# The decay chain of a complex linear attention: the multiply im/re moved to VectorE, a clamp dropped, the 1e-6 term taken into the log scan, the phase rounded on ScalarE

## The chip, the cores and the metric

The kernel runs on one core of a Trainium2 chip. The metric is the device time of one execution in microseconds (us), the median of several runs. The core has four compute engines with a queue each, worked off in order: TensorE (PE; its weight loads are listed as PEld), VectorE (DVE), ScalarE (ACT) and GpSimd (POOL). SyncE (SP) issues the DMAs. Engines wait for each other by semaphores.

## What is computed

The input is a linear attention with a complex decay for every position, head and dimension (batch 4, 8 heads, 768 positions, dimension 48), followed by a soft mixture of 8 experts and a last layer with a squared ReLU. The part that matters here is the decay:

```python
mag = np.sqrt(a_re * a_re + a_im * a_im)
scale = np.minimum(mag, 0.999) / (mag + 1e-06)
a_re_n, a_im_n = (a_re * scale, a_im * scale)
for t in range(S):
    new_re = ar * S_re - ai * S_im
    new_im = ar * S_im + ai * S_re
    S_re, S_im = (new_re + kv, new_im)
    y[:, :, t] = np.einsum('bhd,bhde->bhe', q[:, :, t], S_re)
```

Then x = y with the heads side by side, logits = x @ phi, a softmax over tokens and one over slots, the experts between them, and relu(x @ w_in)**2 @ w_out.

## The kernel before, in words

**The factored form.** The product of the decays up to a position is written as exp(L) times a rotation by an angle. L is the running sum of log(min(mag, 0.999)/(mag + 1e-6)*mag), the angle the running sum of arctan(im/re). With E = exp(+-L) and W = (cos, sin) of the angle, queries and keys are scaled and rotated once, and the recurrence becomes chunks of 128 positions: scores, a causal mask, a product with v, and a state carried from chunk to chunk. Three flags tell at the end if all decays were in the range of this form; if not, the function `general` runs the recurrence step by step. On these inputs it doesn't run.

**The work.** There are 24 units (u) of 128 positions: 4 batches of 6. The decays are prepared in T groups (v), with dimensions times heads on the partitions and 3 tiles side by side: nine groups, of 1, 2 and 3 units, then six of 3. A group of 3 units works on 128x1152 elements. Its steps are the *T chain* of `plan_t` (lines 797 to 873), in this order: clamp re (D, line 823), Ln (A), Exp with a minus sign, which gives 1/re (A, with a flag), im times 1/re (G, line 826), clamp that to +-1.56 (D, line 827), square (A, line 828), Ln(1+x) (A), square of the square for a flag (A, line 830, aside), log of the magnitude as a weighted sum (D, line 831), 1e-6/magnitude by an Exp (A, line 832), minimum with log 0.999 less that term (D, line 833), running sum L in three scans, held above -65 (D, line 838 through line 836), Arctan (A), running sum of the angle in three scans (D, line 841 through line 836), whole turns as an integer (D, line 843), angle less the turns (D, lines 846 to 849). D, A and G stand for VectorE, ScalarE and POOL. Activations go through the helpers at lines 276 and 291, so these two lines stand for all of them in the profile.

`spans` and `waves` then turn L and the angle by TensorE (line 882), so that positions lie on the partitions, and take Exp, Sin and cos. `plan_u` does a unit: scale q and k by E (line 965, "decay"), rotate them by W (line 971), transpose (line 989), scores (line 1037), mask (line 1041), products with v and the state (lines 1052 and 1057), new state (lines 1014 to 1026). Beside these run the slot sums (`plan_g`) and the conversion of w_in from float64 (`plan_wi`). After it come the experts (lines 527 and 542), then the last layer (lines 660 to 742).

**What sets the order.** In this first part all steps are handed to the class `Plan` (lines 84 to 161), a list scheduler that runs while the program is built. Each step has an engine, a cost, a due time, the steps that it comes after and the buffers that it takes and gives back. The planner plays the engines forward with these costs; of the steps that could start on an engine it issues the one due first. What it issues is the fixed order of each engine's queue on the chip. Some copies may go to ScalarE or VectorE ("AD"); the planner gives them to whichever takes them first, with a late due time on VectorE. Where TensorE has nothing in the plan and two of six PSUM banks are free, it adds a pair of warm-up products (line 1170).

The T chain's due times start at the unit's place, less 1.2 times the sum of the chain's costs, less 10 us, and grow by 1.2 times each step's cost. To each is added a shift from the table `SHIFT`, found by the step's number in the chain and by its group:

```python
D3 = 3 * (0.00104 * w + 0.07)
i = add(eng, cst, start, fn, after=after, ..., tab=kw.get("tab"), key=f"T{k}")
start += cst * SLACK
```

The shifts that matter here: T3 -129.1, T4 -23.5, T5 19.7, T6 26.0, T7 32.2, T8 -43.6, T9 5.8, T10 -193.4, T11 4.8, T12 17.9, T13 25.5, T14 17.2, T15 -1.6; "decay" 8.4. Of the 16 expert weight loads 3 are issued early; the others wait for the buffers that the last T group, the last turn and the last unit give back (lines 1144 to 1152).

Of the kernel before, what the change touches and what calls it, by code (L numbers as in the profile page):

```python
# [11 lines left out]
F32 = mybir.dt.float32  # L12
# [26 lines left out]
AR_MIN, AR_MAX, X_LIM, L_MIN = 1e-5, 1e18, 1.56, -65.0  # L39
# [3 lines left out]
# how much later than their place in the order the steps of a name, or of a T unit, are due  # L43
# [40 lines left out]
class Plan:  # L84
    """Steps of one engine each, issued in the order of a list schedule: a step starts when
    the steps before it are through and its buffers are free, and of those that could start,
    the one due first does. Steps that need another function table count as due HOLD later.
    A step of two engines runs on the one that takes it first, as due SECOND later on the second."""
# [6 lines left out]
    def add(self, eng, cost, due, fn, after=(), get=(), put=(), lat=0.0, tab=None, key=None):  # L95
        """cost: of each of the engines. fn takes the engine where there is a choice."""
        engs = [eng] if eng in ("PE", "SP") else list(eng)
        key = key or fn.__name__
        due += SHIFT.get(key, 0.0) + SHIFT.get(self.group, 0.0)
        self.steps.append((dict(zip(engs, cost if len(engs) > 1 else [cost])), due, fn,  # L100
                           [a for a in after if a is not None], get, put, lat, tab))
        return len(self.steps) - 1

    def issue(self, warm):
# [3 lines left out]
        ready = {"SP": [], "D": [], "A": [], "G": [], "PE": []}  # L108
# [55 lines left out]
def general(ctx, tc, raw, cs, phs, grp, table):  # L164
    """The recurrence step by step, for any decays; then the slot sums again."""
    nc = tc.nc
# [86 lines left out]
def moe_kernel(ctx, tc, raw, cst, aT, qk, vv_d, phi, w1, w2, w_in, w_out, out):  # L253
# [16 lines left out]
    lim = const.tile([128, 2], F32, name="lim")  # L270
# [22 lines left out]
    def grp_steps(g, st, p_s, ps_m):  # L293
        """Slot sums and slot weights of four units: (engine, cost, what, wants) each."""
# [75 lines left out]
    def merge_steps(p_s, ps_m):  # L370
        """The four running slot sums as one, over the sum of the weights."""
# [59 lines left out]
    def combine_steps(p_m):  # L431
        """The slot weights of all tokens from their logits."""
        m = p_m.tile([128, NU], F32, name="m")
        wide = lambda: m.unsqueeze(2).to_broadcast([128, NU, NS])

        def inverse():
            V.tensor_reduce(out=m, in_=cn, axis=AX, op=ALU.add)
            V.tensor_scalar(out=m, in0=m, scalar1=1e-9, scalar2=None, op0=ALU.add)
            V.reciprocal(m, m)
        return [lambda: V.tensor_reduce(out=m, in_=cn, axis=AX, op=ALU.max),  # L440
                lambda: (V.tensor_tensor(out=cn, in0=cn, in1=wide(), op=ALU.subtract), tact(SET_EXP, cn, cn, AF.Exp)),
                inverse,
                lambda: V.tensor_tensor(out=cn, in0=cn, in1=wide(), op=ALU.mult)]
# [5 lines left out]
    def f64_steps(p_d, raw, dst):  # L449
        """float64 as pairs of words (low, high) to float32: (engine, what) each."""  # L450
        shape = list(dst.shape)
        t = {}

        def word(k):
            return raw()[:, :, :, k]

        def fields():
            t["x"] = p_d.tile(shape, U32, name="dx")
            V.tensor_scalar(out=t["x"], in0=word(1), scalar1=3, scalar2=0x3FFFFFF8, op0=ALU.logical_shift_left, op1=ALU.bitwise_and)

        def size():
            t["y"] = p_d.tile(shape, F32, name="dy")
            act(t["y"], word(1).bitcast(F32), AF.Abs)

        def low():
            V.scalar_tensor_tensor(out=t["x"], in0=word(0), scalar=29, in1=t["x"], op0=ALU.logical_shift_right, op1=ALU.bitwise_or)

        def top():
            V.scalar_tensor_tensor(out=t["x"], in0=word(1), scalar=0xC0000000, in1=t["x"], op0=ALU.bitwise_and, op1=ALU.bitwise_or)

        def flush():
            V.scalar_tensor_tensor(out=dst, in0=t["y"], scalar=F64_MIN, in1=t["x"].bitcast(F32), op0=ALU.is_ge, op1=ALU.mult)
        return [("A", size), ("D", fields), ("D", low), ("D", top), ("D", flush)]
# [6 lines left out]
    # expert weights, in the order in which the products take them: of four experts, a quarter  # L480
    # of the hidden columns each
# [11 lines left out]
    def grp_flags(p_f, ps_f):  # L493
        """128 when all decays are in the range of the factored form."""
# [10 lines left out]
    def finish(weights, psum, ps_b, hid, p_raw, p_d, used, swap, check):  # L505
        """The experts on the slot sums, then the last layer. used(n): product n has taken its weights;
        swap: makes room for the last layer's weights when the sixth up product has taken its own."""
# [42 lines left out]
        def warm(n):  # L550
            """Products that keep the array's clock up."""
            for _ in range(n):
                mm(ph_[0][:, :C], ident, ident, start=True, stop=True)
# [28 lines left out]
        def decode(n):  # L582
            """The n-th rows of w_out as float32."""
            R["dw", n] = R["dw"].tile([128, 1, DM], F32, name="dw")
            return [fn for _, fn in f64_steps(p_d, lambda: R["raw", n], R["dw", n])]

        def part(n):
            """The n-th rows of w_out as two parts."""
# [161 lines left out]
    with tc.manual_schedule():  # L750
# [46 lines left out]
        def plan_t(v):  # L797
# [5 lines left out]
            A1, D1, D2, P1 = cost("A", e), cost("D", e), cost("D", e, half=True), e * 0.00223  # L803
            D3 = 3 * (0.00104 * w + 0.07)
# [21 lines left out]
            step("G", P1, lambda: nc.gpsimd.tensor_tensor(out=g("a1"), in0=g("a1"), in1=g("t2"), op=ALU.mult))  # L826
            step("D", D2, lambda: V.tensor_scalar(out=g("a1"), in0=g("a1"), scalar1=X_LIM, scalar2=-X_LIM, op0=ALU.min, op1=ALU.max))
# [5 lines left out]
            step("D", D1, lambda: V.scalar_tensor_tensor(out=g("a0"), in0=g("a0"), scalar=LN_CLIP, in1=g("t3"), op0=ALU.min, op1=ALU.subtract))  # L833
            def sums(out, src, op, low, first):
                for j in range(3):
                    V.tensor_tensor_scan(out=v3(out)[:, j], data0=v3(src)[:, j], data1=low.to_broadcast([128, w]),  # L836
                                         initial=first[:, j:j + 1] if first is not None else 0.0, op0=ALU.add, op1=op)
            step("D", D3, lambda: sums(g("t3"), g("a0"), ALU.max, lim[:, :1], None), put=["a0"], key=("L", v))

            step("A", A1, lambda: tact(SET_TRIG, g("a1"), g("a1"), AF.Arctan), mid=("sq", v), tab=SET_TRIG)  # L840
            step("D", D3, lambda: sums(new("t4"), g("a1"), ALU.add, lim[:, 1:], st.pop(("fl", v - 1)) if c else None),
                 get=["t4"], dep=("fl", v - 1))
            step("D", D2, lambda: V.tensor_scalar(out=g("a1").bitcast(I32), in0=g("t4"), scalar1=1.0 / (2 * math.pi), scalar2=None, op0=ALU.mult))
# [15 lines left out]
            for k, (eng, cst, fn, kw) in enumerate(seq):  # L859
# [4 lines left out]
                if eng == "G":  # L864
                    after.append(ids["a1", v])
# [26 lines left out]
        def spans(v, due):  # L892
            """E+ and E- of the units of v, and the decay over all of v."""
# [210 lines left out]
        V.memset(lim[:, :1], L_MIN)  # L1104
        V.memset(lim[:, 1:], 0.0)
# [76 lines left out]
        def used(k):  # L1182
            supply(n + N_POST + k)
# [65 lines left out]
```

## Time and profile before

| | us |
|---|---|
| three runs | 581.35, 582.32, 584.56; median 582.32 |
| profiled execution: span from its first to its last instruction | 578.5 |
| TensorE busy | 540.0 (93%) |
| VectorE busy | 453.5 (78%) |
| ScalarE busy | 373.7 (65%) |
| POOL busy | 44.7 (8%) |

The times of the runs include what lies around the span; of the profiled execution only the span is known. An engine counts as busy while an instruction of its own runs, so an instruction that is held up by another engine's use of memory also counts as busy. A window row gives, for a stretch, the busy us of each engine with the number of instructions in brackets, then the share of TensorE's full clock that was granted, and the DMA's share.

### The profile page before, as it was taken

Reading aid. Unit: us, or ns where it says so; the run is one execution under the profiler, and the core shown is the slowest. Engines: PE = TensorE matmul, PEld = TensorE weight load, DVE = VectorE, ACT = ScalarE, POOL = GpSimd, SP = SyncE. Lnnn points to the kernel's source line nnn. Section 1 sums busy time; section 2 is a strip of 40 time slices with the busy share of each in tenths; the row PEclk is TensorE's granted clock in tenths of the full one; section 3 lists DMA queues with packets and bytes.
Section 4 is the critical chain, followed back from the end, with each engine's and each line's share of the span. In section 5 each row is a group of like instructions: output and inputs, shape, how many; then the busy total and the mean of one; then the engine's idle time right before and its main releaser. Section 6 shows DMA issues by size and latency. Waiting matters only on the chain. (4 is left out here: it accounts for less than half of the span.)

```text
span 578.5 us, 10970 instructions
## 1 busy us (share of the span) xinstructions
PE 540.0 (93%) x4368; PEld 473.5 (82%) x4368; DVE 453.5 (78%) x743; ACT 373.7 (65%) x687; POOL 44.7 (8%) x28
## 2 busy tenths in 40 slices
PE   2989999999998989999999997789999999999995
PEld 2978788878787878887844987679999999999995
DVE  3979899999999999998648799866666666666662
ACT  6878788889798868783214678455555555555552
POOL 1111020012001020000000133210000000000000
PEclk9989899999999989999999998899999999999998
DMA  8762323343415223498996133010010100100101
GB/s 308 292 249 83 109 87 120 117 131 113 134 42 159 77 68 111 134 390 320 386 374 228 54 110 110 1 55 1 1 55 1 54 2 1 56 0 2 55 1 60
DMA packets 24827, 67.29 MB, mean 116 GB/s; under 512 B 2240, under 2 KB 15424, under 8 KB 22720
## 3 DMA queue, kind: packets, MB, share of 16 engines
q1 hardware_dynamic: 24768, 66.51, 33.3%
q8 instruction: 36, 0.59, 0.4%
q14 instruction: 23, 0.19, 0.1%
HBM read 61.78 MB, written 4.72 MB: 115 GB/s over the span
## 5 line engine op out<-in xcount | busy, mean ns | idle before, releaser
L727 PE MATMUL po<-woh,sh 128*128 128x384 f32 x384 | 131.7, 343 | 5.7 <-ACT sh L276 5.7
L727 PE MATMUL po<-wol,sh 128*128 128x384 f32 x384 | 130.6, 340 | 0.0
L276 ACT ACTIVATE sh<-s 128x512 fp32r<-128x512 f32 x96 | 60.6, 632 | 71.6 <-DVE s L684 71.2
L695 DVE TENSOR_TENSOR sl<-s,sh 128x512 fp32r<-128x512 f32 x81 | 56.1, 693 | 55.6 <-ACT sh L276 34.7
L724 PE MATMUL po<-woh,sl 128*128 128x384 f32 x384 | 86.8, 340 | 0.7 <-POOLq L1192 0.7
L727 PEld LDWEIGHTS po<-woh,sh 128*128 128x128 f32 x384 | 73.0, 190 | 9.1 <-ACT sh L276 8.4
L727 PEld LDWEIGHTS po<-wol,sh 128*128 128x128 f32 x384 | 72.9, 190 | 3.8
L684 DVE TENSOR_TENSOR s<-s 128x512 f32<-128x512 f32 x85 | 60.0, 706 | 14.6 <-ACT s L276 14.5
L724 PEld LDWEIGHTS po<-woh,sl 128*128 128x128 f32 x384 | 69.5, 189 | 1.3 <-POOLq L1192 1.1
L276 ACT ACTIVATE s<-ph 128x512 f32<-128x512 f32 x96 | 56.9, 593 | 17.6 <-PE ph L680 17.3
L276 ACT ACTIVATE T<-pt 96x512 f32<-96x512 f32 x81 | 45.3, 592 | 19.5 <-PE pt L989 19.0
L1170 PE MATMUL pt<-cs 128*128 128x128 f32 x284 | 41.9, 300 | 11.7 <-DMA cs<-in_const_dram 11.5
L1037 PE MATMUL pt<-T,T 96*128 96x128 f32 x384 | 52.0, 282 | 0.0
L1170 PEld LDWEIGHTS pt<-cs 128*128 128x128 f32 x284 | 38.1, 211 | 13.9 <-DMA cs<-in_const_dram 11.5
L1037 PEld LDWEIGHTS pt<-T,T 96*128 96x128 f32 x384 | 46.2, 192 | 3.5 <-issue 3.0
L1052 PE MATMUL py<-am,v 128*48 128x128 f32 x384 | 41.4, 294 | 2.5 <-DVE am L1041 2.5
L680 PE MATMUL ph<-cT,G 128*128 128x512 f32 x96 | 40.0, 416 | 0.3 <-ACT s L276 0.2
L826 POOL TENSOR_TENSOR a<-a,t 128x1152 f32<-128x1152 f32 (+2 forms) x9 | 24.3, 2699 | 183.5 <-ACT t L291 167.4
L836 DVE TENSOR_TENSOR_SCAN t<-a,lim 128x384 f32<-128x384 f32 (+2 forms) x39 | 36.7, 995 | 0.2 <-ACT a L291 0.2
L1041 DVE TENSOR_TENSOR am<-pt,cs 128x512 f32<-128x512 f32 x48 | 32.7, 682 | 4.3 <-PE pt L1037 3.7
L695 POOL TENSOR_TENSOR sl<-s,sh 128x512 fp32r<-128x512 f32 x15 | 20.2, 1347 | 151.6 <-ACT sh L276 146.6
L1057 PE MATMUL py<-T,S 96*48 96x128 f32 x320 | 31.9, 277 | 0.0
(155 smaller groups left out, 936.2 us busy)
## 6 DMA issues: line engine op xcount, KB each, us to landing
w<-in_w_dram SPq DMA_DIRECT2D x16, 1536.0 KB, 9.3
qk<-in_qk_dram SPq DMA_DIRECT2D x24, 384.0 KB, 3.2
a<-in_a_dram SPq DMA_DIRECT2D x14, 576.0 KB, 4.1
raw<-in_wi_dram SPq DMA_DIRECT2D x16, 384.0 KB, 4.4
raw<-in_wo_dram SPq DMA_DIRECT2D x16, 384.0 KB, 3.2
v<-in_vn_dram SPq DMA_DIRECT2D x24, 192.0 KB, 2.4
out_dram<-o SPq DMA_DIRECT2D x24, 192.0 KB, 2.0
a<-in_a_dram SPq DMA_DIRECT2D x2, 384.0 KB, 6.0
```

What stands on the lines that cost most here:

```text
L276: return nc.scalar.activation(*args, **kw)
L680: mm(p, G[:, 128 * f:128 * (f + 1)], R["cT", g], start=True, stop=True)
L684: V.tensor_tensor(out=s, in0=s, in1=s, op=ALU.mult)
L695: (nc.gpsimd if 0 < n < 16 else V).tensor_tensor(out=sl, in0=s, in1=sh, op=ALU.subtract)
L724: mm(po[t][:, :DM], sl[:, C * t:C * (t + 1)], R["woh"][:, f], start=False, stop=f == 15)
L727: mm(po[t][:, :DM], sh[:, C * t:C * (t + 1)], R[w][:, f], start=f == 0 and w == "woh", stop=False)
L836: V.tensor_tensor_scan(out=v3(out)[:, j], data0=v3(src)[:, j], data1=low.to_broadcast([128, w]), initial=first[:, j:j + 1] if first is not ...
L1037: mm(p[:, C * h:C * (h + 1)], st["T", u, 1, g][:, h], st["T", u, 0, g][:, h], start=True, stop=True)
L1041: V.tensor_tensor(out=m, in0=st["pa", u, g].rearrange("p (h t) -> p h t", h=4), in1=cs[:, C_CAUS:C_CAUS + C].unsqueeze(1).to_broadcast([12 ...
L1052: mm(p[64 * w:64 * w + D, C * pr:C * (pr + 1)], st["v", u][:, h], st["am", u, h // 4][:, h % 4], start=True, stop=fst)
L1057: mm(p[64 * w:64 * w + D, C * pr:C * (pr + 1)], st["S", u][:, h], st["T", u, 0, h // 4][:, h % 4], start=False, stop=True)
L1170: mm(p[:, :C], ident, ident, start=True, stop=True)
```

## The change

The multiply im * (1/re) is a VectorE instruction instead of POOL's. The clamp of the quotient to +-1.56 is gone; values out of that range are told by the flag of the fourth power, as before. The term 1e-6/magnitude is no longer subtracted together with the minimum; the minimum is a one-input instruction, and the scan of the logs subtracts the term as its second operation, reading it from the tile that it writes (in place of the lower limit of -65). The whole turns are computed by a ScalarE copy with a scale and an integer output. The planner's cost of a scan is changed, and its queue for POOL and the constant tile with the limits go. The chain has 15 steps in place of 16, so the later steps have other numbers; the table `SHIFT` is as it was.

```diff
-AR_MIN, AR_MAX, X_LIM, L_MIN = 1e-5, 1e18, 1.56, -65.0
+AR_MIN, AR_MAX = 1e-5, 1e18
...
-        ready = {"SP": [], "D": [], "A": [], "G": [], "PE": []}
+        ready = {"SP": [], "D": [], "A": [], "PE": []}
...
-            A1, D1, D2, P1 = cost("A", e), cost("D", e), cost("D", e, half=True), e * 0.00223
-            D3 = 3 * (0.00104 * w + 0.07)
+            A1, D1, D2 = cost("A", e), cost("D", e), cost("D", e, half=True)
+            D3 = 3 * (0.0021 * w + 0.05)
...
-            step("G", P1, lambda: nc.gpsimd.tensor_tensor(out=g("a1"), in0=g("a1"), in1=g("t2"), op=ALU.mult))
-            step("D", D2, lambda: V.tensor_scalar(out=g("a1"), in0=g("a1"), scalar1=X_LIM, scalar2=-X_LIM, op0=ALU.min, op1=ALU.max))
+            step("D", D1, lambda: V.tensor_tensor(out=g("a1"), in0=g("a1"), in1=g("t2"), op=ALU.mult), needs=("a1", v))
...
-            step("D", D1, lambda: V.scalar_tensor_tensor(out=g("a0"), in0=g("a0"), scalar=LN_CLIP, in1=g("t3"), op0=ALU.min, op1=ALU.subtract))
-            def sums(out, src, op, low, first):
+            step("D", D2, lambda: V.tensor_scalar(out=g("a0"), in0=g("a0"), scalar1=LN_CLIP, scalar2=None, op0=ALU.min))
+
+            def sums(out, src, op, less, first):
                 for j in range(3):
-                    V.tensor_tensor_scan(out=v3(out)[:, j], data0=v3(src)[:, j], data1=low.to_broadcast([128, w]),
+                    V.tensor_tensor_scan(out=v3(out)[:, j], data0=v3(src)[:, j], data1=less(j),
                                          initial=first[:, j:j + 1] if first is not None else 0.0, op0=ALU.add, op1=op)
-            step("D", D3, lambda: sums(g("t3"), g("a0"), ALU.max, lim[:, :1], None), put=["a0"], key=("L", v))
+            step("D", D3, lambda: sums(g("t3"), g("a0"), ALU.subtract, lambda j: v3(g("t3"))[:, j], None), put=["a0"], key=("L", v))
...
-            step("D", D3, lambda: sums(new("t4"), g("a1"), ALU.add, lim[:, 1:], st.pop(("fl", v - 1)) if c else None),
+            step("D", D3, lambda: sums(new("t4"), g("a1"), ALU.add, lambda j: zero.to_broadcast([128, w]), st.pop(("fl", v - 1)) if c else None),
                  get=["t4"], dep=("fl", v - 1))
-            step("D", D2, lambda: V.tensor_scalar(out=g("a1").bitcast(I32), in0=g("t4"), scalar1=1.0 / (2 * math.pi), scalar2=None, op0=ALU.mult))
+            step("A", A1, lambda: act(g("a1").bitcast(I32), g("t4"), AF.Copy, scale=1.0 / (2 * math.pi)))
...
-                if eng == "G":
-                    after.append(ids["a1", v])
+                if "needs" in kw:
+                    after.append(ids[kw["needs"]])
```

## Rows read from the trace of the kernel before

**Rows 1.** The span and the mean granted clock, core by core.

```profile
core 0: 578.5 us, clock 0.982
```

**Rows 2.** Two windows: busy us (count) of each engine, granted clock, DMA share, GB/s.

```profile
core 0: us, PE busy (x) PEld busy (x) DVE busy (x) ACT busy (x) POOL busy (x), PEclk, DMA share, GB/s
...
60.00:280.00 220.00, 213.63 (x2178) 176.67 (x2177) 208.00 (x329) 176.18 (x331) 15.85 (x5) 0.98 0.45 148
```

**Rows 3.** The same two stages, instructions of line 1170 alone: PE and PEld.

```profile
20.00:60.00 40.00, 18.82 (x131) 17.02 (x129) 0.95 0.56 198
...
60.00:280.00 220.00, 7.98 (x50) 6.83 (x51) 0.98 0.45 148
```

**Rows 4.** Waits of TensorE, 20 to 280 us: us in total, times, longest us.

```profile
PE pt L882 <- DVE t L836: 5.1, 7, 2.1
PE py L1052 <- DVE am L1041: 2.5, 4, 1.7
PE pt L1073 <- DVE am L1041: 1.5, 1, 1.5
PE pt L989 <- DVE KN L971: 1.0, 1, 1.0
PE pt L989 <- DVE QN L971: 0.5, 1, 0.5
```

**Rows 5.** Timeline of POOL: start us, us, instruction; first and last of nine multiplies.

```profile
8.65 1.00 POOL L826 TENSOR_TENSOR a<-a,t 128x384 f32<-128x384 f32 x1 [8.19 <-ACT t L291]
...
204.54 3.73 POOL L826 TENSOR_TENSOR a<-a,t 128x1152 f32<-128x1152 f32 x1 [28.93 <-ACT t L291]
```

**Rows 6.** Timeline of VectorE: three instructions beside POOL's multiply and three like them.

```profile
13.02 2.63 DVE L836 TENSOR_TENSOR_SCAN t<-a,lim 128x128 f32<-128x128 f32 x3 [0.21 <-ACT a L291]
...
17.96 1.05 DVE L836 TENSOR_TENSOR_SCAN t<-a,lim 128x128 f32<-128x128 f32 x3
...
60.60 0.16 DVE L904 TENSOR_TENSOR ecr<-en,cs 128x24 f32<-128x24 f32 x1
...
130.10 0.94 DVE L965 TENSOR_TENSOR qke<-qk,E 128x768 f32<-128x768 f32 x1
...
141.03 1.62 DVE L965 TENSOR_TENSOR qke<-qk,E 128x768 f32<-128x768 f32 x1
...
205.72 2.59 DVE L904 TENSOR_TENSOR ecr<-en,cs 128x24 f32<-128x24 f32 x1
```

**Rows 7.** After the last multiply: TensorE's timeline, then a window with the clock.

```profile
209.03 0.42 PE L1052 MATMUL py<-am,v 128*48 128x128 f32 x4 [1.71 <-DVE am L1041]
...
210.50:214.00 3.50, 3.50 (x23) 3.11 (x24) 3.50 (x7) 1.80 (x4) 0.00 (x0) 0.59 0.19 56
```

**Rows 8.** Groups of VectorE by line and shape: busy us, mean ns | idle before.

```profile
L831 DVE SCALAR_TENSOR_TENSOR a<-t,a 128x1152 f32<-128x1152 f32 x7 | 9.4, 1348 | 0.0
...
L833 DVE SCALAR_TENSOR_TENSOR a<-a,t 128x1152 f32<-128x1152 f32 x7 | 9.4, 1346 | 0.0
...
L823 DVE TENSOR_SCALAR a<-a 128x1152 f32<-128x1152 f32 x7 | 5.3, 752 | 0.0
L843 DVE TENSOR_SCALAR a<-t 128x1152 int32<-128x1152 f32 x7 | 5.2, 749 | 0.0
L827 DVE TENSOR_SCALAR a<-a 128x1152 f32<-128x1152 f32 x7 | 5.2, 743 | 0.0
```

**Rows 9.** Groups of ScalarE by line and shape: the square of line 828.

```profile
L276 ACT ACTIVATE t<-a 128x1152 f32<-128x1152 f32 x7 | 8.2, 1174 | 0.3 <-DVE a L827 0.3
```

**Rows 10.** Timeline of VectorE: a log scan group and the first decay product after it.

```profile
144.71 2.64 DVE L836 TENSOR_TENSOR_SCAN t<-a,lim 128x384 f32<-128x384 f32 x3
...
150.44 0.95 DVE L965 TENSOR_TENSOR qke<-qk,E 128x768 f32<-128x768 f32 x1
```

**Rows 11.** Timelines: first late weight load (SyncE), then the experts' first product (TensorE).

```profile
241.15 0.33 SPq L491 DMA_DIRECT2D w<-in_w_dram  x1
...
291.16 0.39 PE L527 MATMUL pt<-w,siT 128*4 128x256 f32 x2
```

More of the change, by code (lines that the diff above doesn't have):

```diff
@@ L269, in moe_kernel @@
     count = const.tile([1, 1], I32, name="count")
-    lim = const.tile([128, 2], F32, name="lim")
+    zero = const.tile([128, 1], F32, name="zero")
     ident = cs[:, C_ID:C_ID + 128]
@@ L1103, in moe_kernel @@
         ids["cs"] = add("SP", 1.0, 3, start, lat=1.9)
-        V.memset(lim[:, :1], L_MIN)
-        V.memset(lim[:, 1:], 0.0)
+        V.memset(zero, 0.0)
         py = ps_y.tile([128, 512], F32, name="py")
```

## The prediction

> **What bounds the kernel now.** I read the span first, then the busy time by stage, then who waited for whom on TensorE, then the two engines that the change unloads. The span is 578.5 us [rows 1]; the three runs' median of 582.32 us lies 3.8 us above it, and I take that surround as unchanged, so every term below is added to the median.
>
> The change touches only the T chain, inside the attention part that comes before the experts; the experts' first product starts at 291.2 us [rows 11]. There two engines are full at once [rows 2]. From 60 to 280 us TensorE is busy for 213.6 of 220 us and VectorE for 208.0, ScalarE for only 176.2 and POOL for 15.9. TensorE's figure is nearly all real work: the warm-up products of line 1170 take 8.0 us of it, against 18.8 us in the 40 us of the ramp before [rows 3]. So TensorE's work is a floor, and the change doesn't alter it. What can be won is the time when TensorE stood still or ran slowly. Its waits on VectorE from 20 to 280 us are 5.1 + 2.5 + 1.5 + 1.0 + 0.5 = 10.6 us [rows 4]; the view has nothing of that size on ScalarE.
>
> Where do these waits come from? POOL runs nine multiplies, of 1.0 to 3.7 us each [rows 5]. Whatever VectorE runs beside one of them is stretched [rows 6]: the first scan group (three of 128) takes 2.63 us, the same group 1.05 us a little later; a decay product takes 1.62 us instead of 0.94; at the last one a 24-element product takes 2.59 us instead of 0.16. Eight of the nine cost VectorE something, 0.67 (the decay product) to 2.42 us, 15.0 us in all. After the last, TensorE stands for 1.71 us until a mask of VectorE arrives, and just behind that the granted clock is 0.59 over 3.5 us [rows 7], which is mostly time at 1.2 GHz where the stretches around it have 2.4 GHz.
>
> **The change part by part.** *Multiply from POOL to VectorE.* Priced like the two-input instruction of line 831: 1.35 us for a full unit [rows 8]. It removes POOL's 24 us, and with them the 15.0 us by which VectorE was stretched. *Clamp dropped:* minus 0.74 us. *Phase to ScalarE:* minus 0.75 us on VectorE. *The 1e-6 term inside the scan:* the two-input instruction of line 833 (1.35 us) becomes a one-input minimum like line 823 (0.75 us): minus 0.59 us [rows 8]. Per full unit VectorE does 1.35 - 0.74 - 0.75 - 0.59 = -0.74 us; seven full units give -5.2 us, the two short ones some -0.9 us by their sizes, together -6.1 us. With the stretching that is about -21 us of VectorE time in a stage where it was full. TensorE is full too, so this is not the gain; the gain is bounded by TensorE's waits.
>
> The Trainium skill (Perfetto Trace Analysis, Optimizing Scalar/DVE Operations) advises the other direction for a saturated VectorE: hand work to ScalarE or even GpSimd, with the caution that GpSimd shares a port with VectorE and may gain nothing. By the advice alone the multiply was free on POOL, nothing of the 15.0 us comes back and the time would stay near 582 to 584 us, where the sum below has 574; rows 6 show the caution at work, so the chance of the advice holding here is small.
>
> *The scan.* Its second input was a broadcast column and becomes a whole tile, read and written in place. No row shows that form. Below nothing is excluded, as it does the same steps on as many elements. Above, one more pass over 384 elements in each of 27 scans, at 0.94/768 us per element of the two-input decay product [rows 6], is 0.47 us each, 12 us or so of VectorE. I take nothing, by the nearest rows: the two-input instruction of line 831 streams 1152 elements from two tiles in 1.35 us [rows 8], 1.2 ns each, while a scan of three times 384 takes 2.64 us [rows 10], 2.3 ns each, so a scan has time for a second stream. Were it 12 us, VectorE would still be 9 us better off than now.
>
> *Phase on ScalarE.* Nine instructions; a full one as the square of line 828, 1.17 us [rows 9], 9.6 us in all. ScalarE has 44 us free in 220 [rows 2], which hides it. What it adds is a handover: the wrap now waits in VectorE's queue for ScalarE, and behind it wait masks and rotations that feed TensorE. Between nothing (the planner put other work in between) and 9 times 1.2 us = 11 us; I take 1 us, because another handover (VectorE waiting for POOL at line 827) goes away at the same time. No DMA is added; the a1 load now gates a VectorE instruction in place of POOL's, and it is issued as before.
>
> *The order.* The plan is made with costs. Its scan cost rises from 1.41 to 2.57 us for a full unit, so its VectorE account per full unit goes from 8.67 to 10.33 us: 13 us more over all units, where the chip has less. And the due-time shifts belong to step numbers: with one step gone each later step takes over its neighbour's shift. Dues relative to the unit's place: the weighted sum of line 831 goes from -67 to +6; the scan of the logs from -15 to -216; the phase from +2 to +10. The extra account can become warm-up products and gaps on TensorE: between nothing and 13 us. The better scan cost (2.64 us measured [rows 10]) speaks for the low end; I take 3 us.
>
> **The sum.** TensorE's waits: between 0 and 10.6 us come back; I take 9.5, as VectorE has over 6 us of slack beyond what these waits hold. Clock: the mean granted clock of 0.98 over 220 us [rows 2] stands for up to 4.4 us; I take 3 us, since the dip in rows 7 follows directly on such a wait. Against it 1 us and 3 us. 582.3 - 9.5 - 3 + 1 + 3 = 573.8, so 574 us. The rest follows as a block: the late weight loads start when the last T chain is through, the first at 241.2 us [rows 11], so they come earlier with it, and the expert and last stages are TensorE's own work in a fixed order. What is late next: TensorE itself, at its floor. Nothing is costed at zero but the scan and ScalarE's busy time; if ScalarE's cover were gone, the 9.6 us would show.
>
> **The rivals.** *The order gives it back (slower).* In the plan the sum of line 831 is now due 6 us behind the place of the unit that needs it; before, the latest step on the way to the log scan was due at about its place. So the decay terms come some 6 us later. How much room is there? In one group the log scan ends at 147.4 us and the first decay product that needs it starts at 150.4: 3 us [rows 10], the first of four groups read in the same view that have 3 to 4.5 us. If the lateness is over 3 to 4 us, TensorE runs dry in four groups; with a further 1 us for the handover each costs about 4 us, 16 us in all; less 12.5 us gained that is +4 us, 586 us, and up to 590 us if more warm-up products come with it. For it: the shifts are plainly fitted to the old numbering. Against it: steps after line 831 are now due at once, and VectorE has 21 us more room to catch up.
>
> *TensorE's floor swallows it (same).* TensorE's waits are taken over by other causes: VectorE would be free earlier, but the units still come at TensorE's pace, and 9 us of gain is lost to warm-up products put in by the larger VectorE account: 580 to 584 us. It would also come out so if POOL's multiply were not what held TensorE up: VectorE -6.1 us, TensorE unchanged (the advice of the Trainium skill's Perfetto Trace Analysis, Optimizing Scalar/DVE Operations, taken without its caution; 0.03 of this rival's chance). For it: TensorE busy 213.6 of 220. Against: the waits of rows 4 are on VectorE, and rows 7 follow a POOL multiply directly.
>
> *More than I count (faster still).* The ramp, with 18.8 us of warm-up products [rows 3], is led by the T chain. If it shortens by 4 us and nothing is given back, 582.3 - 10.6 - 4.4 - 4 gives 563 us.
>
> *The change doesn't do what it says:* the POOL multiply is surely gone, so I give this nothing of its own.
>
> **How the numbers follow.** Half a per cent, 2.9 us, is about what a measurement of this kernel can tell from no change. Forecast (566 to 579 us) 0.52, faster still 0.08, floor 0.17, order 0.23. So faster 0.60, same 0.17, slower 0.23. The likeliest case's own range is 566 to 579 us; the range that should hold 8 in 10 reaches from 565 us, leaving out most of the faster-still case, to 587 us, leaving out the worse half of the order case.
>
> **What would show it.** Right: no POOL instruction before 320 us; 24-element products all near 0.17 us; VectorE's waits in TensorE's list under 3 us; clock 1.00 in the stage after 60 us; the first expert product some 8 us earlier than now [rows 11]. The scan is right if three of 384 take 2.6 us, wrong at 3.5 or more. The handover is wrong if VectorE is listed as waiting for ScalarE at the wrap for more than a few us. The order rival shows as TensorE waiting for the transposes of the log scan (line 882) or for rotations (line 989), or as line 1170 over 40 us before 291 us. The forecast is wrong if TensorE's real work is as early as before while the stage doesn't end sooner.

## The result, and the profile after

The changed kernel takes **589.58 us** (median of 4 runs, 589.06 to 590.05), beside 581.84 us for the kernel before, run next to it. The ratio is 1.0126, 95% interval 1.0087 to 1.0165: slower by 1.3%, where 574 us was forecast. Its profiled span is 588.3 us, 9.8 us more than before.

Almost everything on which the forecast rested is there. The stage of 60 to 280 us, in the view of rows 2:

```profile
60.00:280.00 220.00, 216.68 (x2206) 181.51 (x2206) 195.40 (x319) 185.55 (x327) 0.00 (x0) 1.00 0.42 138
```

POOL is silent, VectorE is busy for 12.6 us less, the granted clock is 1.00. TensorE's waits from 20 to 280 us, the view of rows 4, in full:

```profile
PE pt L343 <- ACT T L276: 0.7, 1, 0.7
PE pt L1169 <- DVE ec L917: 0.5, 1, 0.5
PE py L1052 <- ACT yT L276: 0.5, 1, 0.5
PE py L1052 <- DVE yT L279: 0.4, 1, 0.4
PE pt L1073 <- ACT E L291: 0.4, 1, 0.4
PE pt L1169 <- DVE am L1041: 0.3, 1, 0.3
PE pt L1073 <- ACT xn L276: 0.2, 1, 0.2
PE pt L882 <- DVE xn L279: 0.2, 1, 0.2
```

The 10.6 us of waits on VectorE have become 1.4 us (0.5 + 0.4 + 0.3 + 0.2). Groups of VectorE up to 330 us, four of the T chain and the 24-element product (mean ns before the second bar):

```profile
L836 DVE TENSOR_TENSOR_SCAN t<-a,t 128x384 f32<-128x384 f32 x21 | 18.4, 936 | 0.0
...
L826 DVE TENSOR_TENSOR a<-a,t 128x1152 f32<-128x1152 f32 x7 | 9.5, 1352 | 0.8 <-ACT t L291 0.7
...
L836 DVE TENSOR_TENSOR_SCAN t<-a,zero 128x384 f32<-128x384 f32 x9 | 7.9, 937 | 0.0
...
L832 DVE TENSOR_SCALAR a<-a 128x1152 f32<-128x1152 f32 x7 | 5.3, 751 | 0.1
...
L904 DVE TENSOR_TENSOR ecr<-en,cs 128x24 f32<-128x24 f32 x9 | 1.6, 180 | 0.6 <-ACT en L291 0.6
```

The multiply costs 1.35 us, the minimum 0.75 us, the scan with a second tile 0.936 us beside 0.937 us with a broadcast column, and the 24-element products average 0.18 us. But the experts' first product, which [rows 11] had at 291.2 us, starts here:

```profile
300.38 0.39 PE L527 MATMUL pt<-w,siT 128*4 128x256 f32 x2
```

It comes 9.2 us *later*. TensorE didn't wait in the sense of the list; it was kept busy. Its books up to that product, all instructions first and then the warm-up products alone (line 1170 before, 1169 after):

```profile
0.00:291.16 291.16, 268.02 (x2642) 225.84 (x2643) 261.53 (x428) 221.99 (x407) 24.50 (x13) 0.98 0.50 172
0.00:291.16 291.16, 41.95 (x284) 38.08 (x284) 0.98 0.50 172
```

```profile
0.00:300.38 300.38, 283.93 (x2817) 242.48 (x2819) 250.68 (x431) 239.22 (x415) 0.20 (x4) 1.00 0.49 168
0.00:300.38 300.38, 63.73 (x460) 57.52 (x460) 1.00 0.49 168
```

The third column is the first run of the next section, which has the changed instructions in the old order:

| TensorE up to the experts' first product, us | before | changed | changed, old order |
|---|---|---|---|
| warm-up products | 41.95 | 63.73 | 40.06 |
| all other products | 226.07 | 220.20 | 222.32 |
| idle | 23.14 | 16.45 | 16.08 |
| the experts' first product starts | 291.16 | 300.38 | 278.46 |
| from there to the end of the span | 287.3 | 287.9 | 287.8 |

So the whole difference arises before the experts. In the changed kernel 21.8 us of warm-up products came in; 6.7 us of idle time and 5.9 us of the other products' time, at a clock of 1.00 in place of 0.98, went out. Whether the added products cost that time or fill it is asked below. ScalarE's table loads up to 300 us tell that the order itself is another one; first the kernel before, then the changed one. (Copies that may go to either engine also moved: VectorE does 38 of them up to 330 us in place of 25, 20.8 us in place of 13.8.)

```profile
L286 ACT ACT_TABLE_LOAD x23 | 29.5, 1283 | 1.1 <-PEq L1240 0.7
```

```profile
L286 ACT ACT_TABLE_LOAD x35 | 44.9, 1283 | 1.3 <-PEq L1239 0.8
```

### The profile page after: what moved, and what is told of

Same layout as the page of the kernel before. It is cut to its first block, busy times and chain, and to the rows that moved or that the text cites. A ratio compares the mean times of both kernels' runs of the same rounds, so it can differ in the third digit from the quotient of the medians.

```text
span 588.3 us, 11319 instructions
## 1 busy us (share of the span) xinstructions
PE 554.7 (94%) x4544; PEld 489.0 (83%) x4544; DVE 442.6 (75%) x746; ACT 391.1 (66%) x695; POOL 20.4 (3%) x19
## 5 line engine op out<-in xcount | busy, mean ns | idle before, releaser
L1169 PE MATMUL pt<-cs 128*128 128x128 f32 x460 | 63.7, 289 | 13.1 <-DMA cs<-in_const_dram 12.0
L1169 PEld LDWEIGHTS pt<-cs 128*128 128x128 f32 x460 | 57.5, 199 | 17.4 <-DMA cs<-in_const_dram 12.0
L684 DVE TENSOR_TENSOR s<-s 128x512 f32<-128x512 f32 x85 | 60.0, 706 | 14.6 <-ACT s L276 14.5
L1014 PEld LDWEIGHTS pS<-v,KN 128*96 128x96 f32 x320 | 29.2, 165 | 3.6 <-issue 3.2
```

The source lines that it names most:

```text
L684: V.tensor_tensor(out=s, in0=s, in1=s, op=ALU.mult)
L1169: mm(p[:, :C], ident, ident, start=True, stop=True)
```

## The experiments

All times below are medians. Each ratio is to the kernel before, run next to it on the same chip; its own median went from 579.5 to 582.0 us from chip to chip, so a difference between runs of different chips can be off by some 2.5 us. A figure in brackets is the ratio's 95% interval.

### Is it the instructions or their order?

The kernel before, with its plan (steps, engines, costs, shifts) untouched; only what the steps issue is exchanged (the minimum and the scan of the logs too, not printed):

```diff
-step("G", P1, lambda: nc.gpsimd.tensor_tensor(out=g("a1"), in0=g("a1"), in1=g("t2"), op=ALU.mult))
+step("G", P1, lambda: V.tensor_tensor(out=g("a1"), in0=g("a1"), in1=g("t2"), op=ALU.mult))
-step("D", D2, lambda: V.tensor_scalar(out=g("a1"), in0=g("a1"), scalar1=X_LIM, ...))
+step("D", D2, lambda: None)
...
-step("D", D2, lambda: V.tensor_scalar(out=g("a1").bitcast(I32), in0=g("t4"), ...))
+step("D", D2, lambda: act(g("a1").bitcast(I32), g("t4"), AF.Copy, scale=1.0 / (2 * math.pi)))
```

> The changed instructions in the order of the kernel before: the planner gets the old 16 steps, costs and shifts (the multiply still planned as POOL's, the dropped clamp planned but nothing issued, the phase planned as VectorE's), and only what is issued differs; 142 warm-up products and 26 table loads, as before. Theory (the loss is the new order): TensorE's 10.6 us of waits on VectorE and the dips of the clock go, so 568 to 573 us. Rival (the instructions themselves cost the time: VectorE waits for ScalarE at the wrap, ScalarE is fuller): 580 us or more, with VectorE's wait for ScalarE at line 846 over 5 us.

Measured: **567.39 us, ratio 0.977 (0.970 to 0.984)**. The same instructions, in the old order, are 2.3% faster than before; in the new order 1.3% slower. The order alone is worth 22 us, and the table above shows it in TensorE's books as 23.7 us of warm-up products. The stage of 60 to 280 us and the experts' first product of this run:

```profile
60.00:280.00 220.00, 216.60 (x2262) 178.63 (x2264) 196.33 (x339) 177.21 (x333) 0.00 (x0) 1.00 0.48 164
```

```profile
278.46 0.39 PE L527 MATMUL pt<-w,siT 128*4 128x256 f32 x2
```

### Which half of the change gains?

Two kernels split it, both in the old order: the multiply alone on VectorE, and all the rest with the multiply left on POOL.

> The kernel before with one edit: the multiply is issued on VectorE, at the place where the planner puts POOL's, order untouched; clamp, subtraction and phase as before. VectorE takes 10.9 us more and is freed of 15.0 us of being held up. If the holding up by POOL is what TensorE waited for: 568 to 574 us. If it is VectorE's load in all (here 4 us less, against 21 us): 578 to 582 us.

> The other half in the old order: clamp dropped (planned, nothing issued), minimum and subtraction parted, phase on ScalarE, but the multiply stays on POOL. VectorE has some 17 us less to do and is still held up nine times. If the holding up is what counts: 577 to 583 us. If VectorE's load does: 568 to 573 us.

Measured: multiply only **568.37 us, 0.977 (0.973 to 0.981)**; the rest only **575.64 us, 0.988 (0.983 to 0.992)**. With the multiply alone VectorE stays nearly as busy as in [rows 2], 205.7 us in place of 208.0 (448.5 in place of 453.5 us over the whole span), and yet 13.5 us are won (581.82 - 568.37):

```profile
60.00:280.00 220.00, 215.53 (x2247) 177.96 (x2249) 205.65 (x350) 171.69 (x327) 0.00 (x0) 1.00 0.48 164
```

So being held up by POOL is what TensorE paid for. The edit also ends VectorE's waits for POOL's result, but in the trace before there is only one, of 2.5 us at the first multiply (line 827, at 9.7 us). The rest wins 6.2 us with POOL's multiply still there, and landed between the two expectations: VectorE's load counts as well, at about half the size. Both together win 14.6 us in the first run, less than the 13.5 + 6.2 = 19.7 of the two alone; presumably they repair partly the same waits, which no run separates.

### Are the added warm-up products the loss?

In `warm`, with the planner's clock at hand, the product isn't issued while the plan goes on as if it were:

```diff
+            if not hid and plan.now >= 60:
+                return True
             p = hid[0] if hid else ps_t.tile([128, 512], F32, name="pt")
```

> The changed kernel, its plan untouched, but the warm-up products that the planner adds after its own time 60 are not issued until the last PSUM banks are handed over (134 in place of 230 in the program). Leaves out: 96 products whose result nobody reads. Theory A (the added products take TensorE's time, 0.21 us each): up to 20 us come back, 570 to 576 us. Theory B (they only fill waits that the new order has anyway): 586 to 590 us, and TensorE's waits for ScalarE and VectorE take their place in the trace.

> The changed instructions in the old order, without the warm-up products after the planner's time 60 until the last PSUM banks are handed over (124 in place of 142; leaves out 18 products that nobody reads, 3.9 us of TensorE). If TensorE is at its floor in the old order: 563 to 565 us. If they only fill waits, as in the changed kernel: 566 to 569 us.

Measured: **591.44 us, 1.020 (1.012 to 1.029)** in the new order, no gain from 96 products fewer. Up to the experts' first product, at 300.6 us, TensorE spends 26.8 us less on warm-up products (63.7 to 37.0, 0.28 us for each of the 96), is idle for 13.5 us more (16.5 to 30.0), and its other products take 13.4 us more (220.2 to 233.6):

```profile
60.00:280.00 220.00, 203.22 (x2001) 166.13 (x2001) 193.50 (x316) 185.12 (x326) 0.00 (x0) 0.94 0.42 138
```

So about half of the products filled waits that the order has anyway. The other half was lost again to the granted clock, 0.94 in place of 1.00; what the order would take without the products at the full clock is not shown. In the old order the same edit, only 18 products, gives **564.55 us, 0.970 (0.967 to 0.973)**, 2.8 us better than the first run, at a clock of 1.00 (60 to 280 us): 6.0 us fewer warm-up products bring the experts 3.4 us earlier (278.5 to 275.0 us), so there about half of them take TensorE's time. This is the fastest version of this study, 3.0% under the kernel before.

### Which number of the planner?

The changed kernel with its own plan, and one number put back in each: the shifts by operation instead of by step number; the old scan cost; both of these; the weighted sum's shift alone; and, not put back but raised, the time by which a step with the other table is held back.

```diff
-i = add(eng, cst, start, fn, ..., key=f"T{k}")
+i = add(eng, cst, start, fn, ..., key=f"T{k if k < 4 else k + 1}")
```

```diff
-D3 = 3 * (0.0021 * w + 0.05)
+D3 = 3 * (0.00104 * w + 0.07)
```

```diff
-i = add(eng, cst, start, fn, ..., key=f"T{k}")
+i = add(eng, cst, start, fn, ..., key="T7x" if k == 7 else f"T{k}")
...
+    ... "T9": 5.8, "T7x": -43.6, "W1": 0.7, ...
```

```diff
-    LAG, LOAD, HOLD, KEEP, T_WARM, SECOND = 0.2, 1.28, 31.3, 0.43, 10.0, 325.2
+    LAG, LOAD, HOLD, KEEP, T_WARM, SECOND = 0.2, 1.28, 100, 0.43, 10.0, 325.2
```

> The changed kernel, but each step of the T chain keeps the due-time shift of its operation (the steps behind the dropped clamp are looked up one number higher). Its program has 212 warm-up products and 36 table loads in place of 230 and 38. If the renumbered shifts are the cause: 575 us or less. If the planner's new scan cost and the new engines' accounts are: 584 to 590 us.

> The changed kernel with the planner's old cost of a scan (1.41 in place of 2.57 us for a full unit). Its program has 182 warm-up products and 30 table loads in place of 230 and 38. If the larger VectorE account of the scans makes the added products: 579 us or less (48 products at 0.21 us are 10 us). If the renumbered shifts alone do: 586 us or more.

> The changed kernel with each operation's own shift and the old scan cost at once; what is left of the new order is the missing step, the engines of multiply and phase and their costs. 30 table loads and 214 warm-up products in the program (old order 26 and 142, changed 38 and 230). If the two edits add up (8.4 and 7.2 us): 574 us. If any order made anew loses what the fitted one has: 578 us or more. By table loads alone, 1.06 us each as the fifth run had it: 4 more than the old order, 572 us.

> The changed kernel with one number of the planner changed: a step that needs the other table counts as due 100 in place of 31.3 us later. 28 table loads and 200 warm-up products in the program, in place of 38 and 230. By table loads at 1.06 us each: 579 us. If the later due times of the steps held back cost as much: 586 to 592 us.

> The changed kernel with one shift only put back: the weighted sum of line 831 (830 in the changed kernel) is due with -43.6 in place of +32.2; all others as in the changed kernel. 34 table loads and 212 warm-up products in the program. This is the step that the prediction's rival named. If it is what makes the decay terms late: 581 us or less, as with all shifts kept (581.2). If it is another of the shifts or the scan cost: 585 us or more.

Measured, with the changed kernel at 589.6:

| edit | us | ratio to before (interval) |
|---|---|---|
| all shifts by operation | 581.15 | 0.999 (0.995 to 1.002) |
| the weighted sum's shift alone | 581.47 | 1.000 (0.997 to 1.002) |
| old scan cost | 582.42 | 1.002 (0.999 to 1.005) |
| both (all shifts, scan cost) | 584.43 | 1.004 (1.001 to 1.006) |
| hold 100 | 585.33 | 1.007 (1.005 to 1.010) |

One shift is worth as much as all of them, 8 us: the step that the prediction's slower rival named. But no edit reaches 567. All shifts and the old scan cost were expected at 575 and 579 us or less by one theory, at 584 and 586 us or more by the other; both landed between. The two together are no better than one: the gains don't add, which speaks against any sum of causes by planner numbers. Hold 100, with 10 table loads fewer, also landed between its expectations (579, and 586 or more).

### Are the added table loads the loss?

In the old order, 12 loads more (the other table and this one again, at six switches); in the new order, 12 loads fewer (`left_out` has the numbers of twelve switches), then also without the warm-up products.

```diff
+            if twice[0] in (5, 8, 11, 14, 17, 20):
+                for m in (n, SET_EXP + SET_TRIG - n):
...
```

```diff
+            if switch[0] in left_out:
+                return
...
+        if n == SET_TRIG and switch[0] in left_out:
+            args = args[:2] + (AF.Abs,)
```

> The changed instructions in the old order, as in the first run, with 12 more table loads on ScalarE and nothing else: at six of the switches, spread over the T chains, the other table and this one are loaded once more. 35 loads in place of 23 before the experts, as the changed kernel has; 12 at 1.28 us are 15.4 us of ScalarE. If ScalarE has become the engine that counts: 575 to 582 us, 8 us or more over the first run's 567.4. If ScalarE's free time (43 us of 220 in the first run) takes them: 567 to 570 us.

> The changed kernel in its own order, without 12 of its table loads: at six places the switch to the table of Sin and Arctan and the switch back are not issued, and the steps between run as Abs, so the cosines and sines of these places are left out (26 loads in the program in place of 38; the 230 warm-up products stay). If the added loads are what the new order costs, as the fifth run had them in the old order (1.06 us each): 575 to 579 us. If the order loses its time to other lateness and the loads fit into waits: 585 to 590 us. In between if the warm-up products, which now fill no wait, hold TensorE up in their place.

> The same, and the warm-up products after the planner's time 60 not issued either, as in the second run (134 in the program). If loads and products together are the whole loss of the new order: 565 to 570 us, what the old order gives. If the order is late by itself: 578 us or more.

Measured: **580.08 us, 0.997 (0.995 to 1.000)** with 12 loads more in the old order, 12.7 us over the first run, 1.06 us for a load of 1.28. ScalarE appears at the head of TensorE's waits, where the first run has 1.3 us on ScalarE in all:

```profile
PE pt L1044 <- ACT T L277: 5.0, 3, 2.7
```

That looked like the answer, and it wasn't: 12 loads fewer in the new order give **589.15 us, 1.017 (1.010 to 1.023)**, and without products as well **588.87 us, 1.018 (1.011 to 1.024)**, both at the changed kernel's own time. A cost that is real in one order is nothing in another. (The last run's clock is 0.95 from 60 to 280 us, so it is to be held against the 591.44 us of the run without products.) In the last of these runs, with loads and products out of the way, TensorE's waits lie open; its timeline between 90 and 110 us (all that waited):

```profile
94.79 0.67 PE L1060 MATMUL py<-am,v 128*48 128x128 f32 x4 [4.05 <-ACT yT L279]
108.98 1.09 PE L997 MATMUL pt<-cs,QN 128*96 128x128 f32 x4 [4.43 <-DVE QN L979]
```

(Lines 1060 and 997 there are 1052 and 989 of the changed kernel.) The first waited for the output bank, whose copy stood on ScalarE behind the E steps of a group that had just become ready; the second for a rotation, which had the cosines of the same late group to wait for.

### Late groups

What is late can be read from the decay products of VectorE (line 965), one a unit. The changed kernel first, then the run with the old order; the 15th and the 16th decay product in both, with the weighted sum (line 830 after, 831 before) and the log scan of the group that the 16th belongs to:

```profile
162.90 0.95 DVE L965 TENSOR_TENSOR qke<-qk,E 128x768 f32<-128x768 f32 x1
163.77 1.35 DVE L830 SCALAR_TENSOR_TENSOR a<-t,a 128x1152 f32<-128x1152 f32 x1
...
170.28 2.65 DVE L836 TENSOR_TENSOR_SCAN t<-a,t 128x384 f32<-128x384 f32 x3
...
181.66 2.65 DVE L836 TENSOR_TENSOR_SCAN t<-a,zero 128x384 f32<-128x384 f32 x3
184.22 2.63 DVE L836 TENSOR_TENSOR_SCAN t<-a,t 128x384 f32<-128x384 f32 x3
...
187.34 0.95 DVE L965 TENSOR_TENSOR qke<-qk,E 128x768 f32<-128x768 f32 x1
```

```profile
154.84 1.35 DVE L831 SCALAR_TENSOR_TENSOR a<-t,a 128x1152 f32<-128x1152 f32 x1
...
161.57 2.65 DVE L836 TENSOR_TENSOR_SCAN t<-a,t 128x384 f32<-128x384 f32 x3
...
164.58 0.95 DVE L965 TENSOR_TENSOR qke<-qk,E 128x768 f32<-128x768 f32 x1
...
172.94 0.95 DVE L965 TENSOR_TENSOR qke<-qk,E 128x768 f32<-128x768 f32 x1
```

For 24.4 us no unit is begun, where the old order takes 8.4. The weighted sum is late already: it starts 0.9 us behind the 15th decay product, in the old order 9.7 us ahead of it, and its shift is the one that won 8 us above. The log scan is over at 172.9 us in the changed kernel; ScalarE does this next:

```profile
173.01 1.28 ACT L286 ACT_TABLE_LOAD   x1
174.31 1.17 ACT L291 ACTIVATE a<-a 128x1152 f32<-128x1152 f32 x1
...
176.05 1.15 ACT L291 ACTIVATE a<-a 128x1152 f32<-128x1152 f32 x1
...
178.02 1.28 ACT L286 ACT_TABLE_LOAD   x1
179.31 1.16 ACT L291 ACTIVATE t<-a 128x1152 f32<-128x1152 f32 x1
...
181.26 0.19 ACT L291 ACTIVATE en<-t 128x3 f32<-128x3 f32 x1
181.36 1.99 ACT L291 ACTIVATE E<-pt 128x384 f32<-128x384 f32 x5
```

Two Arctans, of this group and of the next, and an Exp of the next group's chain stand ahead of the E that the unit needs; from the scan's end to the first E 8.5 us pass. In the old order 1.1 us pass:

```profile
165.30 1.64 ACT L291 ACTIVATE E<-pt 128x384 f32<-128x384 f32 x4 [0.58 <-PE pt L882]
```

Then two scans of the next group (181.7 and 184.2 us) stand ahead of the decay product on VectorE. The log scans of two groups are also nearly together here (the steps "en" right behind them at 181.3 and 187.9 us; 164.5 and 194.8 us in the old order). I took that for the cause and kept the groups apart by one dependence:

```diff
+                if k == 1 and v > 2:
+                    after.append(ids["L", v - 1])
```

> The changed kernel with one dependence more in the plan: from the fourth T group on, the first Ln of a group comes after the log scan of the group before, so that two chains don't run abreast. 38 table loads and 240 warm-up products in the program, as many as or more than the changed kernel's 38 and 230. If pairs of groups abreast (log scans 3.8 and 6.6 us apart in the changed kernel) starve TensorE: 576 to 582 us, and no gap over 20 us between decay products in the trace. If the loads and the products were the loss after all: 588 us or more.

Measured: **586.99 us, 1.010 (1.006 to 1.015)**. The pairs are gone (85.6 and 107.4 us, 179.9 and 201.3 us), and the gaps are not: 22.9 us is now the longest. Groups abreast are not the cause of the gaps; the edit won 2.6 us. What all these runs share is the gap itself. The longest stretch without a decay product is 13.6 to 14.4 us in the six kernels with the old order (the one with added loads too) and 16.1 to 34.7 us in the others. But its length doesn't tell the time: 16.1 us with both numbers put back (584.43 us), 22.0 us with all shifts by operation (581.15 us).

### One true account at a time

Last from the other side: the old plan with the changed instructions (567.4 us), and one of the planner's accounts made true in each run. The planner's cost of a scan (the edit of D3 above, the other way round) was also changed alone in the kernel before.

```diff
-step("G", P1, lambda: V.tensor_tensor(out=g("a1"), in0=g("a1"), in1=g("t2"), op=ALU.mult))
+step("D", D1, lambda: V.tensor_tensor(out=g("a1"), in0=g("a1"), in1=g("t2"), op=ALU.mult))
```

```diff
-step("D", D2, lambda: act(g("a1").bitcast(I32), g("t4"), AF.Copy, scale=1.0 / (2 * math.pi)))
+step("A", A1, lambda: act(g("a1").bitcast(I32), g("t4"), AF.Copy, scale=1.0 / (2 * math.pi)))
```

> The changed instructions in the plan of the first run (old steps, shifts and costs), but the multiply is planned as what it is, a VectorE step of 1.26 us in place of POOL's of 2.57. 34 table loads and 228 warm-up products in the program (first run 26 and 142). If any step planned anew loses the fitted order: 577 us or more, about 10 us over the first run's 567.4. If the shifts and the scan cost alone carry the loss: 567 to 571 us.

> As the run before, but the phase alone is planned as what it is, a ScalarE step of 1.05 us in place of VectorE's of 0.66; the multiply is planned as POOL's again. 36 table loads and 234 warm-up products. If any step planned anew loses the fitted order: 577 us or more. If not: 567 to 571 us.

> As the first run, but the planner has the new cost of a scan (2.57 in place of 1.41 us for a full unit), all else of its plan old. 32 table loads and 206 warm-up products. From the fourth run, where the old cost gave 7 us back: 574 to 577 us. If any order made anew loses the fitted one's whole advantage: 579 us or more.

> The kernel before with nothing but the planner's cost of a scan changed as in the changed kernel (1.41 to 2.57 us for a full unit). 32 table loads and 206 warm-up products in the program, in place of 26 and 142; instructions as before. If a cost in the planner alone costs time on the chip: 587 us or more (6 loads at 1.06 us). If the truer cost gives a truer order: 576 to 581 us.

| made true in the plan | us | ratio to before (interval) | over 567.4 |
|---|---|---|---|
| nothing | 567.39 | 0.977 (0.970 to 0.984) | |
| the multiply | 589.24 | 1.015 (1.010 to 1.019) | 21.9 |
| the phase | 593.02 | 1.023 (1.018 to 1.028) | 25.6 |
| the scan cost | 584.05 | 1.006 (1.004 to 1.009) | 16.7 |
| the scan cost, kernel before | 582.63 | 1.004 (1.001 to 1.006) | |

Each of the three, alone, loses as much as the whole change or nearly, with the same instructions on the chip and the shifts untouched. So the loss belongs to no one account. The reading that fits is that the old order is a fitted one: the shifts hold for the list of steps, engines and costs that they were fitted to. That is inferred; no run fitted the shifts again. What is measured is that every plan with one of these changed lost 14 to 26 us against 567.4. In the kernel before, where POOL still holds VectorE up, the true scan cost moves the time by 0.4% only, where 587 us or more and 576 to 581 us had been expected. There TensorE's books to the experts have 15.8 us more of warm-up products (57.8), but 6.7 us less idle time and 6.9 us less for the other products, at a clock of 1.00: so the new order adds products there too, but in the place of waits and of low clock.

What stays open is why the other orders all lose so much: late E and cosines at the head of groups are seen in the traces, one shift accounts for 8 us, and the rest was not located.

## Why the prediction was wrong

**The mechanism was right, and its size nearly so.** The terms for TensorE's waits (9.5 us) and the clock (3 us), less 1 us for the handover, make 11.5 us; in the old order the change gave 14.6 us. TensorE's books there have 7.1 us less idle time, 3.7 us less for the other products at the higher clock and 1.9 us fewer warm-up products before the experts. POOL's hold-ups were 15.0 us of VectorE and the multiply alone, moved, won 13.5. VectorE's busy time fell by 18.6 us in the old order (453.5 to 434.9), where some 21 was worked out. The scan's second input cost nothing (0.936 against 0.937 us), the wrap waited for ScalarE 2.4 us in all, inside its bounds of 0 to 11.

Three readings were wrong without harm to the sum. "Whatever VectorE runs beside one of them is stretched" is too wide: beside the multiply that holds up the decay product of 1.62 us [rows 6], two masks, which read TensorE's banks, keep their time. The decay product at 204.86 us also keeps its 0.94 us, beside the multiply that took 3.73 us.

```profile
138.26 3.58 POOL L826 TENSOR_TENSOR a<-a,t 128x1152 f32<-128x1152 f32 x1 [17.56 <-ACT t L291]
...
139.36 0.69 DVE L1041 TENSOR_TENSOR am<-pt,cs 128x512 f32<-128x512 f32 x1
...
140.43 0.68 DVE L1041 TENSOR_TENSOR am<-pt,cs 128x512 f32<-128x512 f32 x1
```

The surround is not 3.8 us: the changed kernel's profiled execution took 590.05 us with a span of 588.3. And the due times of before leave out 2 us that the code adds to the sum of the costs; they are -70, -17 and 0, not -67, -15 and +2.

The Trainium skill's advice (Perfetto Trace Analysis, Optimizing Scalar/DVE Operations) fails without its caution about the shared port: here the engine with 208 of 220 us busy gained by taking the work back.

**The step that failed is the order, of which the prediction said "I take 3 us".** It measured 22.2 us (567.4 to 589.6). Three things were wrong in it. Its upper end, 13 us, was worked out as VectorE's larger account turned into warm-up products; it left out that a list scheduler with another list gives another order altogether, with late groups. So the sentence that the late weight loads and the experts come earlier failed with it. I took the low end because the scan cost had become truer; truer accounts made a worse order out of the old one in three runs out of three. And "steps after line 831 are now due at once" was counted against the rival, while in the stretch shown above ScalarE's Arctans, whose shift went from 17.9 to 4.8 by their new number, stood ahead of the E steps; that they stood there is seen; that they cost the time is not shown by a run.

**The slower rival came nearest, by part of its reason.** It had the weighted sum of line 831 late by its neighbour's shift, four groups starved, 586 us and up to 590 us; the kernel takes 589.6, and that one shift put back gives 8.1 us. It got 0.23. But the order cost 22.2 us where it had 16, that shift is less than half of it, and three runs lost 16.7 to 25.6 us with no shift renumbered; that its upper end was met is in part luck. The range ended at 587 us, half-way into this case: cutting it there was the second error, since nothing in the profile bounded the order.

**Of the signs named,** POOL's silence, the 24-element products, TensorE's list, the clock and the scans all came out as for the forecast; the experts' first product, which was to come 8 us earlier, came 9.2 us later. So the others tell the instructions, and only this one the order. The rival's sign, line 1170 over 40 us before 291 us, was badly set: the kernel before has 42.0 us already, the changed one 57.4 (34.2 and 49.5 us from 20 us on).

## What to carry to other kernels

Where a list scheduler with fitted due times sets the order, an edit of one step is two changes, of the instructions and of the order; run the new instructions in the old order first (plan the old step, issue the new one), and fit again only then. Truer costs made no better order here while the other numbers stayed as they were for the old ones. A cost measured in one order (a table load here, 1.06 us or nothing) says little of another. And a run that leaves out warm-up products is read with its granted clock beside it.

## What the runs showed of the hardware

A VectorE scan of two tiles in place takes as long as one with a broadcast column (0.936 and 0.937 us for 384 elements). A ScalarE copy of 1152 elements with integer output took 1.15 to 1.23 us in the timeline, like the float square of [rows 9] with 1.17. TensorE with warm-up products in every gap kept a granted clock of 1.00 from 20 to 280 us; with 96 of them left out it was 0.94 from 60 to 280 us, and the other products before the experts took 233.6 us in place of 220.2 (591.4 beside 589.6 us in all). Beside a multiply of POOL, most two-input VectorE instructions out of SBUF were held up (2.59 us in place of 0.16 for 24 elements), while masks that read PSUM kept their 0.68 us; a held-up instruction shows as a longer one, not as a wait.
